# A DeltaNet recurrence with a gelu MLP on one core: the written-out order of all engines, loads, PSUM banks and filler matmuls, planned anew

## The chip, the cores and the metric

The kernel runs on one core of one Trainium2 chip. A core has five engines that each work through a queue of their own: PE (matrix products; loading its weights is shown apart as PEld), DVE (VectorE), ACT (ScalarE), POOL (GpSimd) and SP, which here only issues loads and copies. The metric is the device time of one execution in microseconds (us).

## The reference

A linear attention with a delta rule runs over 768 steps for 4 x 8 heads with 48 channels each; its output, laid out as 3072 tokens of 384 channels, goes through an MLP with a tanh gelu.

```python
k_n = k / (np.linalg.norm(k, axis=-1, keepdims=True) + 1e-06)
for t in range(S):                                  # S = 768
    y[:, :, t] = einsum('bhd,bhde->bhe', q[:, :, t], state)
    v_old = einsum('bhde,bhd->bhe', state, k_n[:, :, t])
    state = state + beta[:, :, t] * einsum('bhd,bhe->bhde', k_n[:, :, t], v[:, :, t] - v_old)
x = y.transpose(0, 2, 1, 3).reshape(3072, 384)
h = x @ w_in                                        # 384 -> 2048
g = 0.5 * h * (1 + tanh(sqrt(2 / pi) * (h + 0.044715 * h**3)))
out = g @ w_out                                     # 2048 -> 384
```

## The kernel before

The 768 steps are cut into 12 chunks of 64. For a chunk, k is squared and summed (`sq`, `ss`), a reciprocal norm is made (`sr`, `rn`), and k is scaled to `Kn` and transposed by PE into `KQT`, beside the transposed q. Products of k with itself and with q give the chunk's triangular matrices (`gram`: `G`, `DT`; `own`: the 16 x 16 and 32 x 32 blocks on the diagonal). The diagonal blocks are inverted by forward substitution in many small instructions (`solve8` on DVE for chunk 0; `solve` on POOL for chunk 1 and then for pairs of chunks), transposed back by DVE (`back`: `TB0`, `TB1`), spread into block matrices (`WB`, `DI`, by `exp`) and joined to the whole inverse `TT` by products (`inverse`: `ET`, then three products one after another). `state` then takes the recurrence one chunk on: `R` = old values minus v, `U` = TT times R, the new state `S`, and the chunk's output, which lands transposed in `x4` ("x" in the text). For most chunks some rows of x are moved by six small DMAs (`xm`).

The MLP works on tiles: chunks 0 to 3 are a tile each, chunks 4 to 11 are taken in pairs (8 tiles, t0 to t7). A first-layer group (`m1`, L1241) fills one PSUM bank by PE, and ACT makes the gelu of it into `gT` (L1243, 128x512). The second layer (`m2`, L1251) is issued in halves of 8 matmuls; its result goes through `osb` to the output by a DMA on ACT's queue.

All of this is recorded as 1277 operations and emitted in an order that is written out by hand in the string `ORDER` at the head of the file. An entry is a letter for the engine and the number of the operation: `p` PE, `v` DVE, `a` ACT, `g` POOL, `s` SP; `p224` is operation 224 on PE, the first MLP group. Some operations may run on either of two engines, and the letter chooses. An entry `w6.7` puts six matmuls on a constant tile `wz` (L414) into PE's queue, writing to PSUM bank 7: filler, whose result is not used. Each engine takes its entries in the order in which they stand in the string, one after another; an entry waits by semaphores for the operations that it reads from, for those whose buffers it overwrites, and, where it takes a PSUM bank, for the last users of that bank. `BANK` gives the bank of each PSUM handle, a digit each. Entries of different engines stand in one string, but only the order within each engine is kept on the chip.

```python
            o = ops[int(w[1:])]
            o.eng, o.end = names[w[0]], n
            assert o.eng in o.fns and o.deps <= seen and o.idx not in seen
            seen.add(o.idx)
            for h, k in o.alloc:
                b0 = self.bank_of[h] = int(BANK[h[1] - 1])
                for b in range(b0, b0 + k):
                    o.sync.update(bank_last[b])
                    bank_last[b] = tuple(self.users[h])
            self.orders[o.eng].append(o.idx)
```

Loads of k, q and v are issued on SP, in order, each behind the reads of the buffer that it fills (three buffers for k and v, one for q); four loads of W1 and four of W2 are issued on POOL, between its compute entries, once q of the first two chunks has landed (`WAFT`), with two more for the rows that hold the fourth part of a head (`W1x`).

Operations that the prediction follows, with their numbers: 61 (transposed beta), 82 and 84 (the two halves of chunk 0's square), 89 and 90 (halves of K0), 66 and 69 (the masks bM of chunks 0 and 1), 152 (own blocks of chunk 0), 156 and 155 (first sums of chunk 0's solve, L846 and L843), 177 (its last transpose), 186 and 187 (DI0), 189 to 203 (chunk 0's inverse on PE), 205 (R0, which reads v of chunk 0, `vf0`), 206 to 212 (its state), 218 and 219 (its x), 224 to 238 (first layer of tile 0), 240 to 246 (its second layer), 307 and 308 (WB of chunk 1), 312 to 326 (its inverse), 398 and 399 (own blocks of chunks 2 and 3), 401 (their transpose `Tt0`), 448 and 466 (first products of their inverses), 349 to 363 (first layer of tile 1), 365 (second layer of tile 1), 510 (of tile 2), 653 (an inverse product of chunk 4). Those numbered 122, 130, 390, 393, 593, 596, 786, 789, 973 and 976 scale k to K.

Of the kernel before, what the change touches and what calls it, by code (L numbers as in the profile page):

```python
# [18 lines left out]
v34 a50 g11 s49 v5 v0 g21 v46 a48 s47 g22 v6 g16 v8 v35 v41 g18 s54 v1 v4 a2 g13 g14 s55 g12 g19 v15 v45 s53 a26 v43  # L19
v33 v10 s56 v3 w6.7 p61 v36 v37 v9 v38 s51 v42 v7 v40 s52 a82 g84 v63 s60 a24 g20 v85 g17 a29 v39 v62 a30 a31 v83 a32  # L20
a23 v67 a86 s59 v70 a87 v64 v88 s57 a97 g75 v89 v65 g81 s58 w12.5 p91 v66 a98 p99 g90 v44 v92 g77 w1.4 p93 a103 v68
p100 v94 g72 g76 a101 s96 p152 v104 g74 v153 g73 a105 w1.7 p181 a106 a182 v107 v154 g108 v156 v155 g69 w8.3 p109 v157
v158 v159 a110 v160 v183 g80 s141 a102 v161 w4.5 p264 v162 v163 v164 p178 v265 a179 v165 g266 v166 a117 v167 v168 v169
v170 a25 a28 g267 a27 v171 g268 g269 v172 g270 g271 v173 g272 g273 v174 g274 g275 v175 g276 g277 v176 a185 g278 g279
s95 a184 v177 w29.3 p191 g280 p301 g281 v192 g282 a187 p189 v186 g283 v190 g284 a188 w1.5 p195 g285 v118 p193 g286
a196 g287 a194 p199 v71 g288 v180 p197 g289 a200 g78 a119 p203 v198 a120 g290 a205 p201 v121 g291 v204 v122 g79 a202
p209 a302 p206 g292 g293 s147 v207 a210 g294 g295 a125 v208 s140 v211 g296 w3.5 p215 v303 p216 g297 p217 s146 p304
v218 a219 p212 p123 v126 a305 g299 v298 a127 a128 v129 a133 v306 g130 v300 s115 v124 a213 s113 g400 w12.7 p131 v308
a309 s116 p398 v132 a311 s114 g603 v214 p399 a250 s111 p314 v401 a310 s112 a315 v251 s144 g402 s142 a375 v307 s143
g403 g404 w10.6 p312 v376 a135 s145 g405 p224 g406 s262 g407 p226 v377 a225 g408 v378 s263 v379 p328 a134 g409 v380  # L30
p228 v381 g410 v382 a313 s151 g411 v329 p136 g412 p137 s150 a229 g413 v383 p316 v138 p318 g414 s149 a317 v384 g415
p438 a227 v385 s223 p230 g416 v386 v139 a439 g417 s222 p232 a231 v387 g418 s148 v388 p320 a233 g419 v389 p459 v319
g390 s220 p234 a460 v440 s221 p322 a235 v321 p456 v461 p324 g420 a323 s396 a457 g393 p326 p441 s397 v327 a519 p236
v325 v458 p333 a442 g421 v520 p238 g422 a334 p391 g423 a253 v443 g424 p330 g425 a239 v331 p338 g426 p394 a252 v332
g427 v335 p339 v392 p340 g428 p341 a578 s259 p342 g429 p240 g430 v344 s260 g431 a343 g433 v579 a395 s258 p254 a237
g432 v580 p601 s345 v437 p602 s261 a444 v434 p241 s346 v462 s347 v604 p255 s348 a242 p349 s436 v256 g605 p351 a350
s435 v581 p644 v582 a352 p466 s531 v583 g521 p353 v584 a645 v585 s532 v445 p245 g522 a354 v646 a257 g606 v586 v587
g607 p355 g608 v464 a467 g609 p336 v588 v446 p448 g610 v337 p246 g611 a449 g612 v589 g613 v463 p523 g614 v590 a356
v591 p474 g615 v592 a247 p450 g690 a447 p357 v451 p359 v475 g593 p524 a360 p452 v525 a358 p468 g616 v453 a526 s599
p361 g596 v469 s600 p454 a362 p363 s527 v455 g617 v691 p476 s530 g618 p470 a477 g619 p480 s529 p594 g620 a364 p481  # L40
s528 g621 p478 a482 g622 p365 v479 s483 g623 a771 g624 s489 v471 p366 g625 s491 a595 v772 g626 s488 g627 g628 p533
a243 v773 s490 p662 v774 g629 p597 a244 v775 s492 g630 v776 p370 g631 a598 v777 s487 v778 g632 v779 g633 v780 s703
a367 g634 p371 v781 g636 v782 a692 s702 v783 v784 v785 g635 p794 v534 a372 a663 p795 v640 g786 a465 p493 v647 p495
v664 a494 g693 p472 v797 a496 p497 s792 g883 p499 v473 a498 s793 v637 p535 v648 s638 g796 p501 a536 v884 s699 p539
a502 p540 p641 g798 s486 v541 p694 a642 s639 p503 a500 v643 s700 g799 p695 a504 g800 p505 v696 g801 s548 p507 a506
s546 v697 p537 a665 s547 p651 g789 p659 v652 p509 s701 a508 s550 v538 a660 g802 p790 s549 g803 a374 p510 v661 g804
s698 a958 g805 v791 s551 g806 a249 v649 p837 g807 p669 v959 s484 p653 a248 g808 s485 p514 g809 a838 v654 g810 a668
g811 v670 a511 p515 g812 g813 v667 v839 g814 p552 g815 v960 a516 v961 p655 g816 v962 a553 p834 g817 v656 p677 a835
g818 p554 v963 g819 a650 v678 p556 g820 a555 g821 p657 v836 a557 g822 p558 v658 a886 g823 v666 g824 p679 g825 a559
# [26 lines left out]
a1276  # L76
"""
BANK = ("6031340340660141100441256766766777042000503073120036766677667154142444144220200367676676760000276766"
        "7676754202240042244430024042067667677676767676767024104052244440000220220666767676767676767661042024"
        "2242042530200022767767667676767676764000444440000044210001203141021031450102")  # L80


# [1257 lines left out]
```

## Time and profile before

| | before |
|---|---|
| time, median of 3 runs | 251.39 us (251.34 to 253.34) |
| profiled execution: span from first to last instruction | 249.4 us |
| profiled execution: time of its own | not given on the page; the median lies 2.0 us above the span |
| PE busy | 232.0 us (93%) |
| DVE, ACT, POOL busy | 161.4, 139.0, 118.6 us |
| mean granted TensorE clock | 0.986 |
| filler matmuls (L414) | 87 |
| HBM read, written | 20.64 MB, 4.72 MB |

The page lists the busy time of each engine, the span in 40 slices of 6.2 us with a digit for tenths of busy time, the granted clock of PE in the same slices, the share of the DMA engines, and the chain of waits, which is followed back from the last instruction. A line of a timeline has start, length, engine, line of the kernel, operation, output and input tiles, and in brackets what ended the idle time before it. A line of a table by stretch has the stretch, its length, then busy time and number of instructions for PE, PEld, DVE, ACT and POOL, the clock, the DMA share and GB/s.

### The profile page before, as it was taken

How to read it: one execution, taken by the hardware profiler on the slowest of the kernel's cores; microseconds unless marked ns; L12 is line 12 of the kernel's file. 1: busy time of each engine (PE TensorE's matmuls, PEld its weight loads, DVE VectorE, ACT ScalarE, POOL GpSimd, SP SyncE). 2: the span in 40 equal slices, each digit the busy share in tenths (PEclk: the TensorE clock that was granted, in tenths of full speed). 3: DMA queues.
4: the chain of work that ended last, by engine and by line, in shares of the span. 5: the costliest groups of instructions: out<-in, count | busy, mean ns of one | idle time of the engine just before them, and what ended most of it. 6: DMA issues, size and time to landing. Idle time of an engine off the chain costs nothing.

```text
span 249.4 us, 12386 instructions
## 1 busy us (share of the span) xinstructions
PE 232.0 (93%) x5637; PEld 155.0 (62%) x5637; DVE 161.4 (65%) x316; ACT 139.0 (56%) x262; POOL 118.6 (48%) x249
## 2 busy tenths in 40 slices
PE   7577896998999799999899999999999999999995
PEld 4334473587778658868766655666656665555562
DVE  6699989886799399896969653767772465100001
ACT  2744578587686466838564357535682247426600
POOL 3685796688389858588045589883000000000000
PEclk9999999799999799999999999999999999999999
DMA  6999969996740825550244000623135210000112
GB/s 157 209 196 168 159 116 211 159 214 107 184 87 19 192 52 112 122 137 7 57 111 91 5 20 23 149 57 63 37 76 134 78 37 3 8 11 32 66 63 96
DMA packets 64789, 23.84 MB, mean 96 GB/s; under 512 B 53600, under 2 KB 63840, under 8 KB 64736
## 3 DMA queue, kind: packets, MB, share of 16 engines
q1 hardware_dynamic: 58656, 14.89, 30.8%
q0 software_dynamic: 1056, 3.15, 7.3%
q10 hardware_dynamic: 5024, 5.02, 6.3%
q8 instruction: 44, 0.72, 1.2%
q14 instruction: 9, 0.07, 0.1%
HBM read 20.64 MB, written 4.72 MB: 102 GB/s over the span
## 4 chain that ended last, share of the span: by engine, by line
PE 81%; DVE 10%; DMA 2%; issue 2%; ACT 2%; POOL 0%; ACTq 0%; POOLq 0%
PE ps L267 76%; DMA kf<-in_k_dram 2%; PE ps L648 2%; PE ps L680 2%; PE ps L414 1%; DVE ss L603 1%; DVE WB L931 1%; ACT WB L915 1%; DVE TB L806 1%; DVE KQT L256 1%; DVE ps L846 1%; DVE Yf L251 1%; DVE Tt L837 1%; DVE btz L251 0%; DVE ps L786 0%
## 5 line engine op out<-in xcount | busy, mean ns | idle before, releaser
L260 ACT ACTIVATE gT<-ps 128x512 bf16<-128x512 f32 x96 | 55.9, 597 | 38.4 <-PE ps L267 36.8
L267 PE MATMUL ps<-x,W 128*128 128x256 bf16 (+1 forms) x384 | 72.2, 329 | 0.0
L267 PE MATMUL ps<-W,gT 128*128 128x384 bf16 x384 | 67.0, 328 | 0.0
L267 PEld LDWEIGHTS ps<-W,gT 128*128 128x128 bf16 x384 | 36.4, 98 | 23.9 <-issue 0.5
L267 PEld LDWEIGHTS ps<-x,W 128*128 128x128 bf16 x384 | 39.1, 115 | 16.3 <-issue 0.3
L762 POOL TENSOR_TENSOR Yf<-Yf,tmp 128x28 f32<-128x28 f32 (+13 forms) x84 | 28.8, 342 | 6.4
L759 POOL TENSOR_TENSOR tmp<-Yf 128x28 f32<-128x28 f32 (+13 forms) x84 | 28.1, 335 | 6.1
L251 DVE TENSOR_TENSOR TT<-ps,DI 128x768 bf16<-128x768 f32 (+2 forms) x30 | 20.2, 684 | 13.8 <-PE ps L267 13.5
L414 PE MATMUL ps<-wz 128*128 128x512 bf16 x87 | 23.3, 416 | 1.4 <-DVE wz L409 1.4
L251 POOL TENSOR_TENSOR Kn<-kf,rn 128x768 bf16<-128x768 f32 (+1 forms) x11 | 16.0, 1452 | 17.1 <-DVE rn L629 10.1
L267 PE MATMUL ps<-KQT 48*32 48x32 bf16 (+1 forms) x1152 | 18.7, 195 | 5.8 <-issue 2.7
L260 ACT ACTIVATE osb<-ps 128x384 f32<-128x384 f32 x18 | 8.8, 490 | 26.3 <-PE ps L267 26.3
L256 DVE COPY osb<-ps 128x384 f32<-128x384 f32 x6 | 3.2, 552 | 29.8 <-PE ps L267 29.8
L260 ACT ACTIVATE G<-ps 128x512 bf16<-128x512 f32 x24 | 14.3, 597 | 11.4 <-PE ps L267 7.7
L267 PEld LDWEIGHTS ps<-KQT 48*32 48x32 bf16 (+1 forms) x1152 | 13.6, 95 | 10.9 <-issue 5.0
L719 DVE TENSOR_TENSOR DT<-ps,mD 128x512 bf16<-128x512 f32 x24 | 16.3, 680 | 4.1 <-ACT G L260 4.1
L267 PE MATMUL ps<-TT,ET 64*64 64x32 bf16 (+1 forms) x768 | 16.4, 176 | 0.0
L267 PEld LDWEIGHTS ps<-TT,ET 64*64 64x64 bf16 x768 | 14.8, 109 | 2.2 <-DVE R L251 0.6
L414 PEld LDWEIGHTS ps<-wz 128*128 128x128 bf16 x87 | 8.7, 105 | 11.5 <-issue 3.0
L251 DVE TENSOR_TENSOR S<-ps,S 128x768 bf16<-128x768 f32 x10 | 9.5, 953 | 9.0 <-PE ps L267 8.9
L260 ACT ACTIVATE x<-ps 128x1024 bf16<-128x1024 f32 (+2 forms) x10 | 9.2, 916 | 8.1 <-PE ps L267 7.9
L251 DVE TENSOR_TENSOR R<-ps,vf 128x768 bf16<-128x768 f32 x11 | 10.4, 949 | 3.8 <-PE ps L267 3.8
(122 smaller groups left out, 333.2 us busy)
## 6 DMA issues: line engine op xcount, KB each, us to landing
qf<-in_q_dram SPq DMA_DIRECT2D x24, 192.0 KB, 4.4
kf<-in_k_dram SPq DMA_DIRECT2D x23, 192.0 KB, 4.9
vf<-in_v_dram SPq DMA_DIRECT2D x40, 96.0 KB, 3.2
out_dram<-osb ACTq DMA_DIRECT2D x16, 192.0 KB, 2.0
W<-in_moe_w_out_dram POOLq DMA_DIRECT2D x4, 384.0 KB, 6.7
out_dram<-osb ACTq DMA_DIRECT2D x16, 96.0 KB, 2.8
W<-in_moe_w_in_dram POOLq DMA_DIRECT2D x4, 192.0 KB, 8.7
vf<-in_v_dram SPq DMA_DIRECT2D x4, 192.0 KB, 11.3
```

The costliest lines, as they stand in the source:

```text
L251: return lambda e: e.tensor_tensor(out() if callable(out) else out, a() if callable(a) else a, b() if callable(b) else b, op)
L256: return lambda e: e.tensor_copy(out, a() if callable(a) else a)
L260: return lambda e: e.activation(out, a() if callable(a) else a, func)
L267: ins = t.matmul(out, lhsT, rhs, start=st, stop=sp_, skip_group_check=skip)
L414: ins = e.matmul(psum[:, b, :], wz[:, 0:128], wz[:, :], start=True, stop=True)
L603: op({"dve": 0.95 * w}, {"dve": lambda e, u=u: e.tensor_reduce(ss[j][:, u], sq[:, u, :], AX.X, ALU.add)}, reads=[f"sq{n}"], writes=[f"ss{j ...
L648: ins = e.transpose(o[:, a, j], Qn[:, n, a, j, :, :].rearrange("q h d -> q (h d)"), identB[:, :])
L680: ins = e.transpose(tb()[:, m, :], t[:, 2 * m:2 * m + 2, :].rearrange("p h d -> p (h d)"), identB[:, :])
L719: op(d_ps(512), {"dve": lambda e: e.tensor_tensor(dv, gview(1)(), md, ALU.mult)}, reads=[h] + MD, writes=[dn])
L759: sop(nb * s * w, lambda e, s=s, w=w, tv=tv: e.tensor_tensor(tv, yf[:, :, s:s + 1, 0:s].to_broadcast([128, nb, w, s]), Yv()[:, :, s + 1:16 ...
L762: sop(nb * s * w, lambda e, s=s, tv=tv: e.tensor_tensor(Yv()[:, :, s + 1:16, 0:s], Yv()[:, :, s + 1:16, 0:s], tv, ALU.add), [YN, TN], [YN])
L806: op({"dve": 0.58}, {"dve": lambda e: e.transpose(dst, src)}, reads=reads, writes=writes)
```

## The change

The strings `ORDER` and `BANK` are replaced. The 1277 operations, their operands and their dependencies stay as they are. What differs:

- the order of the entries on each of the five engines, the places of the loads among them, and the bank of most PSUM handles;
- the engine of 80 operations: 39 go from DVE to ACT, 20 from ACT to DVE, 10 from POOL to DVE, 2 from DVE to POOL, 5 from ACT to POOL and 4 from POOL to ACT;
- the filler: 87 matmuls in entries of 6, 12, 1, 1, 8, 4, 29, 1, 3, 12 and 10 become 68 in entries of 5, 15, 6, 4, 4, 4, 2, 18, 4, 3 and 3.

The string's lines up to about the first group of MLP tile 1, its end, and the banks:

```diff
@@ ORDER
-v34 a50 g11 s49 v5 v0 g21 v46 a48 s47 g22 v6 g16 v8 v35 v41 g18 s54 v1 v4 a2 g13 g14 s55 g12 g19 v15 v45 s53 a26 v43
-v33 v10 s56 v3 w6.7 p61 v36 v37 v9 v38 s51 v42 v7 v40 s52 a82 g84 v63 s60 a24 g20 v85 g17 a29 v39 v62 a30 a31 v83 a32
-a23 v67 a86 s59 v70 a87 v64 v88 s57 a97 g75 v89 v65 g81 s58 w12.5 p91 v66 a98 p99 g90 v44 v92 g77 w1.4 p93 a103 v68
-p100 v94 g72 g76 a101 s96 p152 v104 g74 v153 g73 a105 w1.7 p181 a106 a182 v107 v154 g108 v156 v155 g69 w8.3 p109 v157
-v158 v159 a110 v160 v183 g80 s141 a102 v161 w4.5 p264 v162 v163 v164 p178 v265 a179 v165 g266 v166 a117 v167 v168 v169
-v170 a25 a28 g267 a27 v171 g268 g269 v172 g270 g271 v173 g272 g273 v174 g274 g275 v175 g276 g277 v176 a185 g278 g279
-s95 a184 v177 w29.3 p191 g280 p301 g281 v192 g282 a187 p189 v186 g283 v190 g284 a188 w1.5 p195 g285 v118 p193 g286
-a196 g287 a194 p199 v71 g288 v180 p197 g289 a200 g78 a119 p203 v198 a120 g290 a205 p201 v121 g291 v204 v122 g79 a202
-p209 a302 p206 g292 g293 s147 v207 a210 g294 g295 a125 v208 s140 v211 g296 w3.5 p215 v303 p216 g297 p217 s146 p304
-v218 a219 p212 p123 v126 a305 g299 v298 a127 a128 v129 a133 v306 g130 v300 s115 v124 a213 s113 g400 w12.7 p131 v308
-a309 s116 p398 v132 a311 s114 g603 v214 p399 a250 s111 p314 v401 a310 s112 a315 v251 s144 g402 s142 a375 v307 s143
-g403 g404 w10.6 p312 v376 a135 s145 g405 p224 g406 s262 g407 p226 v377 a225 g408 v378 s263 v379 p328 a134 g409 v380
-p228 v381 g410 v382 a313 s151 g411 v329 p136 g412 p137 s150 a229 g413 v383 p316 v138 p318 g414 s149 a317 v384 g415
-p438 a227 v385 s223 p230 g416 v386 v139 a439 g417 s222 p232 a231 v387 g418 s148 v388 p320 a233 g419 v389 p459 v319
-g390 s220 p234 a460 v440 s221 p322 a235 v321 p456 v461 p324 g420 a323 s396 a457 g393 p326 p441 s397 v327 a519 p236
-v325 v458 p333 a442 g421 v520 p238 g422 a334 p391 g423 a253 v443 g424 p330 g425 a239 v331 p338 g426 p394 a252 v332
-g427 v335 p339 v392 p340 g428 p341 a578 s259 p342 g429 p240 g430 v344 s260 g431 a343 g433 v579 a395 s258 p254 a237
-g432 v580 p601 s345 v437 p602 s261 a444 v434 p241 s346 v462 s347 v604 p255 s348 a242 p349 s436 v256 g605 p351 a350
-s435 v581 p644 v582 a352 p466 s531 v583 g521 p353 v584 a645 v585 s532 v445 p245 g522 a354 v646 a257 g606 v586 v587
-g607 p355 g608 v464 a467 g609 p336 v588 v446 p448 g610 v337 p246 g611 a449 g612 v589 g613 v463 p523 g614 v590 a356
-v591 p474 g615 v592 a247 p450 g690 a447 p357 v451 p359 v475 g593 p524 a360 p452 v525 a358 p468 g616 v453 a526 s599
-p361 g596 v469 s600 p454 a362 p363 s527 v455 g617 v691 p476 s530 g618 p470 a477 g619 p480 s529 p594 g620 a364 p481
-s528 g621 p478 a482 g622 p365 v479 s483 g623 a771 g624 s489 v471 p366 g625 s491 a595 v772 g626 s488 g627 g628 p533
-a243 v773 s490 p662 v774 g629 p597 a244 v775 s492 g630 v776 p370 g631 a598 v777 s487 v778 g632 v779 g633 v780 s703
-a367 g634 p371 v781 g636 v782 a692 s702 v783 v784 v785 g635 p794 v534 a372 a663 p795 v640 g786 a465 p493 v647 p495
...
+v0 g11 s49 a50 v34 v46 g21 g16 s47 a48 g18 v3 g13 v35 v36 v43 g22 v37 v39 s52 v9 v33 g17 g12 v15 v38 v5 s51 w5.5 p61
+s60 v63 v7 v62 v64 g82 v4 v70 g14 s53 g84 v10 v41 s59 v83 v85 v1 v67 s56 v65 a86 a87 s55 a103 v88 g66 v40 v90 g19 g89
+v104 w15.5 p93 s96 p91 a94 s54 v92 a105 v68 s58 p152 a106 v107 v69 v153 g108 v44 s57 v154 v156 w6.5 p109 a110 s140
+v155 g72 a2 s95 a98 w4.5 p264 g20 g97 g73 s141 v265 v157 w4.5 p99 g266 v158 v159 p100 v160 v161 v162 a101 v163 v164
+g267 v165 v166 v167 a102 v168 w4.5 p178 g268 v71 p181 g79 v169 v170 g269 a32 a31 w2.5 p301 a26 g270 v171 a179 g271 a30
+v45 g77 a25 a24 v172 a205 g272 g78 a182 v173 g400 a23 a28 a27 v174 a302 a117 g273 v175 g274 v176 g275 a184 g276 v177
+g277 a185 w18.5 p189 g278 v180 g81 a186 v118 p191 g279 g603 v190 a119 a125 v192 w4.3 p193 g280 a187 g281 v194 g282
+v126 g283 w3.3 p195 g74 p304 v183 p197 g284 g285 v303 a198 g75 a29 a196 p201 a127 g286 a188 p199 g76 a120 a202 a200
+g287 p206 a128 a305 p203 g288 g80 a207 v204 v6 v42 p209 g289 v129 v306 g290 g291 v130 g292 v210 w3.2 p131 v208 g293
+a211 v121 a133 p215 g294 a250 v122 p216 g295 p217 g296 g299 s147 p123 v219 s146 p212 a124 v218 g297 v300 p224 a213
+v132 p228 v298 a225 s115 p398 v309 a308 s114 p399 v251 s113 a214 s116 v310 a229 s112 p232 v401 a375 s111 p226 a307
+v376 p328 g402 p314 a227 s262 a315 p230 v377 g403 v378 a135 g134 p318 v379 v380 v8 p312 v381 a319 v382 g404 s150 p136
+v383 g796 a313 v384 p137 s263 v385 v386 a233 s151 p316 v138 g405 a311 s148 p234 g406 v329 a317 s143 g407 a231 p322
+g408 v139 s149 a235 p320 g409 v387 a323 p459 g410 p438 a460 p236 v388 g411 v389 a439 v461 g412 p326 a321 g413 v390
+a237 p441 v327 p324 s397 v440 g414 a442 p456 p238 g415 s396 a519 v443 g416 p338 v325 a239 g417 p391 a457 g418 p240
+v392 a253 g419 v393 g420 a252 v458 g421 p333 p330 v520 g422 a334 s258 p601 a331 g423 s144 p339 a578 p394 g424 v332
+s260 g425 p241 v395 s142 g426 g427 v335 s145 v579 g428 p340 g429 s261 p341 g430 p342 s259 v580 v242 g431 g433 p602
+v581 a343 v582 a344 p254 v604 g432 p349 p255 a350 g605 v434 p351 a256 s435 p353 s436 v583 a352 v437 g606 p644 s220
+p336 g607 a645 v257 p245 g608 s221 g522 a444 v584 v585 s531 a354 v586 g609 v587 v445 g521 p448 a462 s532 v588 v646
+p355 a449 g610 p246 v446 s529 v589 v337 g611 a356 s528 g612 g981 s530 a465 v590 p466 v463 p474 s222 v464 a467 p450
+v591 v475 s527 g613 p359 s223 g614 v451 p523 a690 g615 p524 g616 v592 v247 a244 p468 g593 a525 p452 p357 v453 a526
+g617 s600 p594 v469 g618 s599 a447 p454 g619 a360 p480 g620 v455 p470 a358 s345 g621 p476 g622 v471 s347 p361 a477
+g623 v691 s346 p363 g624 a362 g625 p478 p481 g626 v479 p365 g627 a482 g628 v596 g629 a771 s702 g692 p533 s491 p472
+a364 v772 g630 s488 p662 g631 a249 p366 s489 a663 g632 v773 s490 v473 g633 a243 v534 g634 s487 a693 g636 p370 s492
+v664 a367 s348 g635 a595 v640 s703 p597 p371 a598 v774 v775 v776 v777 v778 p535 a372 v779 p539 v637 a647 p794 v648
...
@@ ORDER, its end (p1274 a1275 a1276 is the last of both)
-a1238 p1245 a1244 p1247 a1246 p1249 p1251 a1250 p1253 a1122 p1255 a1126 p1257 a1252 a1248 p1259 p1261 a1260 a1254
-p1128 a1256 a1258 p1262 v1129 a1130 p1265 a1263 a1264 p1266 p1269 p1270 p1273 v1271 v1267 a1268 p1274 a1272 a1275
+a1244 p1257 a1238 p1259 a1246 p1251 a1250 a1240 p1247 a1252 p1233 a1258 p1253 a1256 a1234 p1128 a1248 a1118 p1261
+a1122 a1254 a1129 p1265 a1260 a1130 p1269 p1270 p1266 a1271 a1272 p1262 a1267 p1273 v1263 a1264 a1268 p1274 a1275
@@ BANK
-BANK = ("6031340340660141100441256766766777042000503073120036766677667154142444144220200367676676760000276766"
-        "7676754202240042244430024042067667677676767676767024104052244440000220220666767676767676767661042024"
-        "2242042530200022767767667676767676764000444440000044210001203141021031450102")
+BANK = ("6730001422362525257070257666777776000332322323021457677677676004500444302024032067766776762202477777"
+        "6676753302245500045422204042266776767676676777667422034444400252222024002766677767676677777665400004"
+        "4444024302040104767766776766776766764022034242243042021404205713442571031023")
```

## The prediction

> **What bounds the kernel now.** I read the page first: busy time, slices, the chain of waits. Then a table of busy time by stretch, what PE waits for from 48 us on, and the timelines of PE, DVE, POOL and SP ahead of that.
>
> ```profile
> span 249.4 us, 12386 instructions
> ...
> PE 232.0 (93%) x5637; PEld 155.0 (62%) x5637; DVE 161.4 (65%) x316; ACT 139.0 (56%) x262; POOL 118.6 (48%) x249
> ...
> PE   7577896998999799999899999999999999999995
> ...
> PEclk9999999799999799999999999999999999999999
> ...
> PE 81%; DVE 10%; DMA 2%; issue 2%; ACT 2%; POOL 0%; ACTq 0%; POOLq 0%
> ```
> PE is filled from about the eighth slice on, and the chain has no other engine of weight after 43 us. The clock fell to 0.50 twice, 43.25 to 46.66 and 84.20 to 87.60.
>
> ```profile
> 43.10:48.20 5.10, 5.07 (x107) 2.72 (x108) 4.75 (x9) 2.74 (x6) 2.44 (x6) 0.67 0.99 184
> 48.20:69.50 21.30, 20.10 (x580) 16.77 (x580) 16.21 (x38) 15.38 (x29) 14.81 (x31) 1.00 0.81 162
> ```
> ```profile
> PE ps L267 <- issue: 3.7, 5, 1.3
> ```
> The last line is all that the matmuls of 48 to 145 us waited for: five gaps without a releaser, 3.7 us. So the end is set by one moment, that at which PE has real work in unbroken supply, and by what is then left. PE's own timeline shows that 43 to 48 us are not such a moment:
>
> ```profile
> 44.29 3.48 PE L414 MATMUL ps<-wz 128*128 128x512 bf16 x10
> 47.70 0.43 PE L267 MATMUL ps<-WB,G 64*64 64x48 bf16 x16
> 48.07 1.50 PE L267 MATMUL ps<-x,W 128*128 128x256 bf16 x12
> ```
> Ten matmuls on the constant, then one product of chunk 1, then the first MLP group (p224). Its x was ready at 36.8. It stands behind p312, which needs WB1_0 (v307, done 47.02), and DVE was late with that since its previous three entries ran against POOL's masks:
>
> ```profile
> 39.82 2.66 DVE L931 TENSOR_SCALAR WB<-TB,mBs 128x128 bf16<-128x128 bf16 x3
> 46.05 0.98 DVE L931 TENSOR_SCALAR WB<-TB,mBs 128x128 bf16<-128x128 bf16 x3
> ```
>
> **A measure of PE's work.** From the trace's signal times I take each PE entry's spacing from the entry before it, and the lower quartile of its kind as its unhindered time (0.65 us for a first-layer group, 1.30 for half a second-layer group, 0.29 to 0.61 for most attention groups). The 326 entries of real work come to 194.6 us. Before, 14.1 are done when p224 ends (48.92), 32.0 when p349 ends (69.50, first group of MLP tile 1), all at 246.49.
>
> **Part 1, chunk 0 up to its inverse (0 to 28 us): 0.3 to 0.5 us earlier.** Both squares go to POOL: 2 x 0.83 with a select of 0.3 between, from k's landing at 7.03, so the second sum waits until 9.1 instead of 8.0. POOL then has the mask product (1.27) and K0_0, which is done at 12.6 instead of 10.9 (DVE). The own blocks are at 13.9 against 14.28 all the same, as one copy moves to ACT and runs beside DVE's. Then a gain:
>
> ```profile
> 15.78 1.59 DVE L846 TENSOR_TENSOR ps<-Tt 128x256 f32<-128x256 f32 x1
> 17.29 1.48 DVE L251 TENSOR_TENSOR Yf<-Tt 128x256 f32<-128x256 f32 x1
> ...
> 15.24 1.84 POOL L251 TENSOR_TENSOR Kn<-kf,rn 128x768 bf16<-128x768 f32 x1 [0.65 <-DVE rn L613]
> 17.05 1.43 POOL L251 TENSOR_TENSOR bM<-btz,mS 128x512 f32<-128x512 f32 x1
> ```
> Each DVE entry ends 0.3 after the POOL entry that it overlaps; the product of twice the size took 0.69. So 0.45 each is fair, 2.1 us less. But bM1 comes onto DVE in front of them and meets the same POOL entry (13.7 to 15.2), and chunk 1's transpose (0.70) is put ahead of the solve: it starts at 18.95 against 18.80. One entry of 0.68 leaves the solve, a memset (0.38) and a change of sign (0.24) come in: end 25.2 against 25.68, last transpose (v177) 28.1 against 28.41.
>
> **Part 2, chunk 0's inverse and state (28 to 41 us): 4 us later.** DI0_0 (three ACT entries, 0.97) and chunk 3's square (0.83) now stand on ACT ahead of DI0_1: 31.75 against 29.91. Its products alternate between ACT and DVE with five other ACT entries between. On DVE two memsets, a reciprocal, DT1_1 and K3 (0.17, 0.17, 0.25, 0.63, 0.95: 2.2) stand ahead of U0_1, U3_0 of chunk 0. Walked entry by entry with these rows, x is ready at 41.6 against 36.8. On ACT and DVE an entry that needn't wait starts some 0.1 before the last one's end (32.00 behind the 0.38 from 31.72); seven such places make 0.7, so 40.9.
>
> **Part 3, the first MLP group: 7 us earlier.** It and a second one now stand directly behind chunk 0's state product, ahead of the own blocks of chunks 2 and 3 and of chunk 1's inverse, and no filler is behind them. p224 ends at 41.6 against 48.92, with 12.1 of work done against 14.1: credit 7.3 - 2.0 = 5.3. The filler itself (87 to 68 matmuls) gives nothing: ahead of this point it fills waits. The masks bM0, bM1 now run on POOL by 30 us, WB1 on ACT (0.97 each).
>
> **Part 4, 41 to 70 us: 1.5 to 2.1 given back.** ACT now has chunk 1's WB, S3, U and x: from gT0 to ET1_1 stand S3 0.72, gT 0.60, a square 0.83, WB 0.97 twice, gT 0.60, ET 1.09, so p318, which needs ET1_1, starts near 48.4 where PE arrives at 46.5 (with the half clock of 43 to 46.7 in it): 1.9 lost, and 0.2 at p316. 19.4 of work lie from p224 to p349; before, 17.9 from p224 to p349 took 20.6, a loss of 2.7. With the same loss and these waits p349 ends at 41.6 + 19.4 + 2.7 + 2.1 = 65.8; with a loss of 2.1 (chunk 1 no longer holds PE up) at 65.2. Before, the same 31.5 of work were done at 69.0. Gain 3.2 to 3.8; I take 3.5.
>
> **Part 5, the rest: nothing.** The order on PE stays within some ten places. Chunk 2/3's solve on POOL starts later (Tt0 at 47.7 against 45.3), but two of its K products (1.48 each) go to DVE, and WB0 had 6.6 us of slack ahead of p448. Before, from p349 to the end PE lost 177.0 - 162.6 = 14.4 us against its unhindered times, 1.4 of it in the second half-clock stretch; I take the same. The loads: k of chunks 1 to 3 ahead of q, W spread from 15 to 35 instead of 10 to 18 and 31 to 33. The last W1 piece is issued at 33.7; by the row of 8.7 from issue to landing it is there at 42.4, by the slowest, 11.2, at 45, by the quiet ones near 4.6 at 38.3; p224 starts at 40.9, so from nothing to 4 us of wait. I take nothing, since SP issues no load from 20 to 39. vf2 and vf3 move 10 to 18 places back on SP, behind q loads, and land 3 us or more ahead of R. The tail (copy, output DMA) is as before:
>
> ```profile
> 246.51 0.49 ACT L260 ACTIVATE osb<-ps 128x384 f32<-128x384 f32 x1 [7.31 <-PE ps L267]
> 247.03 0.34 ACTq L275 DMA_DIRECT2D out_dram<-osb  x1
> ```
>
> **Sum.** Span 249.4 - 3.5 = 245.9. The page gives no time of its own execution beyond the span; the median 251.39 lies 2.0 above it, and I keep that: 247.9 us.
>
> [...] Eight K products go from POOL to DVE (0.95 instead of 1.48). The row first: POOL's subtraction at 33.14 took 0.77 where its neighbours took 0.23 to 0.25, while such a DVE product ran (32.88 to 33.83). [...]
>
> **Rivals.**
> B, ACT takes the place of the waits (16%). 39 entries go from DVE to ACT, 20 back, four come from POOL. Walked with full row times, ACT is without a gap from 42 to 105 us; the groups p478, p653 and p510 then wait 0.4, 0.4 and 1.1 and others 0.4: 2.3 back, 250.2. For it: the many gelus (0.597) between which short copies must fit. Against: the 0.1 of overlap of part 2, 1.5 us over sixteen entries of such a stretch.
>
> C, vf0 late (18%), the slower side. R0 is now ACT's 21st entry, ahead of chunk 0's G0_1 and of the constants and WB; before, it was the 37th, at 32.36.
>
> ```profile
> 9.90 2.03 SPq L275 DMA_DIRECT2D vf<-in_v_dram  x2
> 12.04 10.31 SPq L275 DMA_DIRECT2D kf<-in_k_dram  x1
> ...
> DMA to landing us min/median/max: 2.5/3.4/18.6
> ```
> vf0 landed at 29.53; the next load's issue hung for 10.31 us while eight W loads were under way. If that repeats, R0 ends at 30.4 instead of 24.0, and everything from WB on shifts by 6.4: 254.3. From a landing at 26.7 on the gain is gone, from 29.2 on it is over 1% slower. Against: only two W1 loads are issued before 20 us, the first at 15.3. Six halves of k and four quarters of q had landed by 13.34; up to and with vf0 three halves more stand in the queue now, some 1.4 each, so 17.5, with W's share 18 to 21.
>
> D, half clock in the thin stretch (8%). From 25 to 31.5 PE has some 1.5 us of work. One more stretch of 3.4 at 0.50 costs up to 1.7, two 3.4: 249.6 to 251.3; I say 250.8. For: the two drops seen. Against: PE stood idle 2.77 at 8.2 to 11.0 at a clock of 1.00. [...]
>
> **How the numbers follow.** Forecast 58%: about 247.9, with parts 1 and 2 uncertain by 2 us either way; three quarters of it lie beyond 1% faster. 1% (2.5 us) is about what a measurement of this kernel can tell from no change. B is mostly within 1%, C slower, D within or slower. Faster 0.48 (0.45 of the forecast, 0.03 of B), same 0.29, slower 0.23. Low end 244.0: the whole credit of 5.3 kept (1.8 more), the second clock drop gone (1.4), and 0.7 of the doubt in part 2. High end 255.0: C, with 0.7 of the same doubt. The forecast's own range is 245.5 to 249.8.
>
> **What would show it.** Right: first MLP matmul at 39.5 to 43 us; no constant matmuls behind 39; v177 near 28; x of chunk 0 at 39 to 42.5, later than before; p318 waiting for ACT; p349 ending near 65.5. Wrong: R's entry on ACT starting behind 26; PE waiting for gT or DMA behind 48 in sum over 3 us more than before; a third clock drop; or p224 held for W.

## The result and the profile after

The changed kernel is slower: 268.81 us median (267.94 to 270.43) against 252.26 us (251.34 to 253.34) of the kernel before on the same chip, a ratio of 1.065 with a 95% interval of 1.057 to 1.072. The profiled execution took 267.94 us, its span is 266.1. Executions of one kernel lie up to 3% apart (264.4 to 272.6 us in the run spread below), in the kernel after the longer ones at a lower granted clock (267.94 us at 0.962, 270.43 at 0.943), so below the time of a kernel is the median of those within 1.5% of its quickest, and the range of all stands behind it. before, measured again beside every group of runs, had medians of 250.8 to 252.9, so 1 or 2 us between kernels of different groups tell nothing.

The page of the kernel after; in its slices a digit is a tenth, and of queue 8, which by the count below brings TensorE's instructions, the line has packets, MB and share of the DMA engines:

```profile
span 266.1 us, 12367 instructions
...
PE 237.0 (89%) x5618; PEld 156.2 (59%) x5618; DVE 150.0 (56%) x302; ACT 151.9 (57%) x303; POOL 109.7 (41%) x242
...
PE   8699678889878699998996989999989999999995
...
PEclk9979999799999799997997799999999999999999
...
q8 instruction: 44, 0.72, 1.1%
...
PE 70%; ACT 12%; DVE 7%; issue 6%; DMA 2%; POOL 2%; SPq 0%; ACTq 0%; POOLq 0%
```
TensorE's share fell from 93 to 89% and does not stay at 9 tenths. The clock now drops to 0.50 in five places (13.6, 47.7, 88.7, 122.8 and 143.3 us), and the chain of waits has 6% of "issue" where it had 2%. The same by stretch, and what TensorE's matmuls waited for from 48 us on:

```profile
48.20:69.50 21.30, 18.59 (x533) 14.36 (x533) 14.45 (x29) 13.76 (x29) 15.10 (x33) 0.93 0.64 138
69.50:88.60 19.10, 14.69 (x456) 11.90 (x454) 14.83 (x28) 14.03 (x27) 14.94 (x30) 1.00 0.65 129
88.60:144.90 56.30, 50.88 (x1564) 38.25 (x1564) 38.85 (x76) 34.85 (x62) 21.47 (x44) 0.93 0.34 73
```
```profile
PE ps L267 <- issue: 11.0, 12, 2.7
PE ps L267 <- DVE S L251: 1.1, 1, 1.1
```
Waits without a releaser ("issue" in the lines: nothing that the profile shows ended them) are 11.0 us in place of 3.7. The two longest, on TensorE's own timeline:

```profile
84.80 1.06 PE L267 MATMUL ps<-x,W 128*128 128x256 bf16 x8
88.51 0.93 PE L267 MATMUL ps<-x,W 128*128 128x256 bf16 x4 [2.65 <-issue]
...
141.67 0.21 PE L267 MATMUL ps<-DI,ET 64*64 64x48 bf16 x1
144.12 1.00 PE L267 MATMUL ps<-DI,ET 64*64 64x48 bf16 x31 [2.24 <-issue]
```
Both stop inside a group: the first behind two matmuls of six of p363, the second behind the first of 32 of p846, and the rest of the group came 2.65 and 2.24 us later, for the same operation. In the kernel an entry's semaphore waits stand ahead of its first instruction, so this is no wait for data. All eleven gaps of over 0.3 us without a releaser behind 43 us stand inside a group, behind 1 to 23 of its matmuls; all eight named ones of over 0.25 us stand ahead of a group's first matmul. I numbered TensorE's weight loads, matmuls and semaphore instructions (some 30 in a run) in order. Each gap of over 0.3 us without a releaser behind 43 us, in both kernels, ends at number 193 + 256n, give or take one: 1985, 2497, 3521, 5825 and 7105 before; those five and 1473, 5313, 6593, 9153 among others after. Queue 8 brings packets of 16384 bytes, 64 for each of 256 instructions, and its n-th packet goes with the n-th of these numbers. In the five gaps of before TensorE went on 1.2 to 1.7 us after the packet's bytes had landed, behind the eleven of after 1.1 to 1.7 us after. The gaps are waits for instructions.

An account of TensorE's time behind 43.1 us, in the measure of the prediction (us; half clock is half of the busy time at 0.50, where a matmul of 512 columns followed its like after 0.427 us, and after 0.216 at 1.00; "rest" is what entries take beyond their unhindered time without a visible gap). The sum of before reaches back to 41.8, where its named gap begins, and 1.2 us of its filler are half clock and stand in both columns, so that its rest is 1.2 more:

| | work | filler | gaps for instructions | named gaps | half clock | rest | sum |
|---|---|---|---|---|---|---|---|
| before | 182.5 | 3.4 | 3.7 | 1.4 | 3.4 | 10.3 | 204.7 |
| after | 181.2 | 0 | 12.6 | 5.0 | 8.1 | 13.2 | 220.1 |

The difference is 15.4 us: 8.9 more for instructions, 4.7 for the clock, 3.6 for named waits and 2.9 of rest, against 4.7 less work and filler behind that point. Set 4 us as what a block of 256 needs (fetch_alone, below, had 3.5 to 4.0): behind the early filler, the blocks with less work than that lack 23.7 us in sum after, 13.4 before; 13 blocks hold under 3 us of unhindered work against 6. The new order bunches attention groups (64 instructions in some 0.3 us).

### The profile page after: what moved, and what is told of

Same layout as the page of the kernel before. It is cut to its first block, busy times and chain, and to the rows that moved or that the text cites. A ratio compares the mean times of both kernels' runs of the same rounds, so it can differ in the third digit from the quotient of the medians.

```text
span 266.1 us, 12367 instructions
## 1 busy us (share of the span) xinstructions
PE 237.0 (89%) x5618; PEld 156.2 (59%) x5618; DVE 150.0 (56%) x302; ACT 151.9 (57%) x303; POOL 109.7 (41%) x242
## 4 chain that ended last, share of the span: by engine, by line
PE 70%; ACT 12%; DVE 7%; issue 6%; DMA 2%; POOL 2%; SPq 0%; ACTq 0%; POOLq 0%
PE ps L267 64%; PE ps L414 2%; PE ps L680 2%; ACT WB L915 2%; DMA kf<-in_k_dram 2%; PE ps L648 2%; ACT gT L260 2%; ACT ET L989 2%; ACT G L260 2%; DVE DT L719 1%; ACT KQT L260 1%; DVE KQT L256 1%; DVE Kn L251 1%; ACT sq L260 1%; DVE sr L626 1%
## 5 line engine op out<-in xcount | busy, mean ns | idle before, releaser
L267 PE MATMUL ps<-x,W 128*128 128x256 bf16 (+1 forms) x384 | 76.9, 343 | 4.0 <-issue 2.7
L762 POOL TENSOR_TENSOR Yf<-Yf,tmp 128x112 f32<-128x112 f32 (+13 forms) x84 | 29.8, 356 | 5.2
L759 POOL TENSOR_TENSOR tmp<-Yf 128x88 f32<-128x88 f32 (+13 forms) x84 | 28.7, 343 | 5.1
L251 POOL TENSOR_TENSOR Yf<-Tt,bM 128x512 f32<-128x512 f32 x5 | 6.4, 1285 | 47.2 <-DVE Tt L875 47.2
L260 ACT ACTIVATE osb<-ps 128x384 f32<-128x384 f32 x17 | 8.3, 492 | 28.1 <-PE ps L267 28.0
L267 PE MATMUL ps<-KQT 48*32 48x32 bf16 (+1 forms) x1152 | 17.9, 194 | 4.5 <-issue 2.7
L414 PE MATMUL ps<-wz 128*128 128x512 bf16 x68 | 19.9, 438 | 1.3 <-DVE pat L421 1.3
L267 PEld LDWEIGHTS ps<-TT,ET 64*64 64x64 bf16 x768 | 14.9, 109 | 3.5 <-issue 2.4
L260 ACT ACTIVATE KQT<-ps 128x1024 bf16<-128x1024 bf16 (+1 forms) x11 | 10.8, 982 | 10.0 <-PE ps L680 6.6
L989 ACT ACTIVATE ET<-ps,mE 128x256 bf16<-128x256 f32 (+1 forms) x30 | 11.4, 452 | 7.2 <-PE ps L267 7.1
L256 DVE COPY KQT<-ps 128x1024 bf16<-128x1024 bf16 (+1 forms) x14 | 9.3, 668 | 11.0 <-PE ps L680 7.2
L915 ACT ACTIVATE WB<-TB,mBs 128x256 bf16<-128x256 bf16 (+1 forms) x36 | 14.2, 464 | 0.0
```

The costliest lines, as they stand in the source:

```text
L251: return lambda e: e.tensor_tensor(out() if callable(out) else out, a() if callable(a) else a, b() if callable(b) else b, op)
L256: return lambda e: e.tensor_copy(out, a() if callable(a) else a)
L260: return lambda e: e.activation(out, a() if callable(a) else a, func)
L267: ins = t.matmul(out, lhsT, rhs, start=st, stop=sp_, skip_group_check=skip)
L414: ins = e.matmul(psum[:, b, :], wz[:, 0:128], wz[:, :], start=True, stop=True)
L759: sop(nb * s * w, lambda e, s=s, w=w, tv=tv: e.tensor_tensor(tv, yf[:, :, s:s + 1, 0:s].to_broadcast([128, nb, w, s]), Yv()[:, :, s + 1:16 ...
```

## Experiments

Theory F says that the supply of instructions and the clock behind it made the loss. Theory D says that operands and banks come late for the new order and the profile fails to name them (it is not rival D of the prediction). An operation behind `p` stands for TensorE's entry of that number; `w1` and three digits are that many matmuls of 48x32 by 32 columns.

**fetch_alone: the supply by itself.** Behind the last matmul of before:

```diff
+ w1512.0 w1512.0                   # 1024 matmuls of 48x32 by 32 columns
+ 6 x (w1112.0 w16.0)               # 112 of them, 16 of 512 columns
+ 4 x (w1104.0 w24.0)
```


> The kernel of before with work for TensorE alone behind its last matmul, on the zero constant: 1024 matmuls of 48x32 by 32 columns in a row (8 blocks of 256 instructions, a weight load and a matmul each); then six blocks of 112 such matmuls and 16 of 512 columns; then four of 104 and 24. Theory F (TensorE's instructions come in blocks of 256 by queue 8, whose 44 packets have 16384 bytes each, and no faster than one in about 3.4 us, the closest that two of these packets started in either trace): the first stretch takes 8 x 3.4 = 27 us or more, with a gap once in each 256 instructions; in the second, 16 x 0.22 + 112 x 0.01 = 4.6 us a block leaves gaps under 0.5 us or none; in the third, 6.3 us a block, none. Theory D (the gaps of the two kernels are waits for operands and banks that the profile fails to name): nothing is waited for here, the 64 matmuls of line 744 took 0.64 us, so the first stretch takes 1024 x 0.01 = 10 us without gaps of a period, 20 us at half clock.

TensorE's timeline, with all other engines at rest but the last output, and then one stretch of the mixed blocks:

```profile
246.82 1.06 PE L427 MATMUL ps<-wz 48*32 48x32 bf16 x107
250.28 1.18 PE L427 MATMUL ps<-wz 48*32 48x32 bf16 x128 [2.39 <-issue]
253.73 1.22 PE L427 MATMUL ps<-wz 48*32 48x32 bf16 x128 [2.27 <-issue]
257.74 1.25 PE L427 MATMUL ps<-wz 48*32 48x32 bf16 x128 [2.78 <-issue]
```
```profile
288.00:297.00 9.00, 9.00 (x257) 4.86 (x256) 0.00 (x0) 0.00 (x0) 0.00 (x0) 1.00 0.02 4
```
128 matmuls and 128 loads in 1.2 us, then 2.3 to 2.8 us of nothing, seven times, at 3.5 to 4.0 us a block; with some 4.5 us of work in a block (9.00 us for the 257 matmuls above) no gap at all. Between 251.8 and 279.1 us the clock stood at 0.50 with nothing on TensorE but these blocks and their gaps. F holds, with a mean of 3.8 us a block in place of 3.4. The three parts of it: behind a block with a wait the next packet starts 1.0 to 1.65 us after TensorE has entered the block ahead of it, takes 0.9 to 1.4, and TensorE goes on 1.2 to 1.55 after it has landed. In the mixed blocks it mostly starts 0.8 to 1.0 after.

**dup_small and dup_wide: the same work, many or few instructions.** On the kernel after:

```diff
- r.append((o, kk, kk, True, True, True))                 # own blocks, dup_small
+ r += [(o, kk, kk, True, True, True)] * 2
```
```diff
+ if gr > 1 and kt == 0:                                  # first MLP layer, dup_wide
+     r.append((<the same output, weights and x>, True, True, True))
```


> The kernel after in which each matmul of the own blocks (line 744, 64 of 32x32 by 32 columns to a group) is issued twice, with the same result: 768 weight loads and 768 matmuls more, in 12 groups. Its first stand in filler; 9 groups lie behind 43 us, where a group took 0.64 us, so that TensorE has 9 x 0.64 = 5.8 us more of work and 1152 more instructions. Theory F (instructions come in blocks of 256, one in 3.5 to 4.0 us at best, as the look with TensorE alone showed): 4.5 more blocks are 16 to 18 us of supply, of which roomy blocks take up some: 9 to 17 us more than 268.8. Theory D (operand waits, wherever the profile has no name for them): 4 to 7 us more.

> The kernel after in which the first matmul of each 256-column output in the first MLP layer of tiles 0 to 3 is issued twice, with the same result: 64 matmuls of 0.107 us, 6.8 us of TensorE work in much the same part of the run as in the run before this one, but 128 instructions in place of 1152. Theory F: the work falls partly into time in which the next block of instructions was awaited anyway: 1 to 5 us more than 268.8. Theory D: 6 to 8 us more, as each matmul adds its own time to a stream that waits for the same operands.

Measured: dup_small 286.2 us in one execution and 291.2 to 293.3 in three, 17 to 24 more than after; dup_wide 266.5 (265.3 to 267.3), 2.4 less, with 6.8 us more of work. Against before in its own group, dup_wide's ratio is 1.062 (1.054 to 1.070) and after's 1.065 (1.057 to 1.072), so no gain is shown, only that the kernel did not get slower. TensorE's busy time and its waits from 43 to 250 us, dup_small above (the execution of 291.2 us), dup_wide below:

```profile
PE 252.1 (87%) x6386; PEld 167.4 (58%) x6386; DVE 149.3 (52%) x302; ACT 152.4 (53%) x303; POOL 108.2 (37%) x242
```
```profile
PE ps L276 <- issue: 20.3, 14, 4.1
```
```profile
PE 244.2 (92%) x5682; PEld 163.6 (62%) x5682; DVE 151.2 (57%) x302; ACT 152.8 (58%) x303; POOL 109.6 (41%) x242
```
```profile
PE ps L276 <- issue: 4.8, 5, 2.1
```
5.8 us of small matmuls raise the waits for instructions to 20.3 us and the half clock to 15; 6.8 us of wide ones lower them to 4.8. D, which expected 4 to 8 us more from each, falls. F's bounds (9 to 17 and 1 to 5 us more) were too narrow on both sides, if only just for the execution of 286.2 us, as they left out the half clock that came with the gaps. dup_wide's 128 more instructions also move the later blocks, which the next run does alone.

**phase: the same stream, shifted by 128 places.** `w1064.5` (64 small matmuls) behind `w15.5`.

> The kernel after with 64 more matmuls (32 columns, constant, no use) behind the second filler, in the 1.5 us that TensorE is idle there: every later instruction stands 128 places further on in TensorE's stream, and nothing else changes. Theory F: gaps without a releaser end at instruction counts 193 + 256n as before, and so in front of other operations: those of 2.65 us ahead of p363 and 2.24 us ahead of p846 are not there, others come; their sum from 43 us on stays within 8 to 17 us (12.6 in the profile after), and the time within 261 to 274 us. Theory D: the same operations wait as long as before, counts 128 higher; time within 1 per cent of 268.8.

264.2 us (262.9 to 265.4). Gaps again end at 193 + 256n, now at other operations (p312, p470, p481, p694, p844, p747); the waits of 2.65 us in p363 and 2.24 in p846 are gone. Their sum is 9.2 us. The operations that waited by D do not wait any more. That 64 useless matmuls gain 4.6 us (ratio to before 1.042, 1.036 to 1.049) also says how much a time here depends on where the blocks fall. dup_wide, which comes to the same shift behind its 64 matmuls, is 2.2 us above phase, 4.9 by the two ratios to before: beside it, the wide work is not free.

**spread and spread_late, bunch, before_even and before_late: rearranged queues.** Each was found by a search over single moves, on the trace's durations and a supply of one block in some 3.7 us. An excerpt of TensorE's queue, spread against after (p569 is an MLP group, p979 and p980 are the own blocks ahead of the gap at 141.88 us):

```diff
- p787 p569 p864 p979 p980 p846 p723 p727
+ p787 p864 p846 p569 p979 p980 p723 p727
```


> The kernel after with the same operations on the same engines and banks; the queues of VectorE, ScalarE, GpSimd and the loads are untouched. Only TensorE's queue is rearranged: about 83 of its 337 entries stand up to 7 places from where they were, so that MLP groups (few and long instructions) lie more evenly between attention groups (many and short). Blocks of 256 instructions that are under 3 us of unhindered work fall from 13 to 7. Theory F: gaps of supply fall from 12.6 to 3 to 6 us and some stretches of half clock with them (8.1 us of cost now): 8 to 14 us less, 255 to 261 us. Theory D: operand waits are what they were, as the other engines do the same in the same order: 265 us or more.

> As the run spread, but TensorE's queue is that of the kernel after up to p349 (69.5 us), so that the early part with its idle stretches and half clock is not touched; only entries behind it are rearranged for an even spread. Theory F: from p349 to the end 193.6 us in the profile after; 186 to 189 us here (the run spread took 187.6), the whole 260 to 264 us. Theory D: 193 us, 267 to 270 us in all.

> The reverse, on the kernel before: only TensorE's queue is rearranged (some 65 of 337 entries, up to a dozen places), so that blocks of 256 instructions with under 3 us of unhindered work rise from 6 to 13, and so that by the durations of the trace no operand or bank is waited for longer in sum. Theory F: gaps of supply rise from 3.7 to about 10 us, and one or two stretches of half clock more: 258 to 266 us. Theory D: 250 to 254 us, as before.

> The kernel before, operations, engines and banks unchanged; the queues of TensorE, VectorE and ScalarE are rearranged by up to a dozen places so that blocks of 256 instructions take more even time and the durations of the trace leave fewer waits. Theory F: gaps of supply (3.7 us) and the half clock behind them mostly go: 246 to 250 us, faster than both kernels. Theory D: 250 to 254 us.

> As the run before_even, but up to p349 (69.5 us) every queue is that of before; only entries behind it are rearranged. Theory F: 2 us of the four gaps of supply behind that point, and the half clock of 84 us with its 1.7 us, go: 248 to 251 us. Theory D: 250 to 254 us.

spread 266.2 (264.4 to 272.6), spread_late 267.1 (one execution, 271.3 to 273.6 in three), before_even 264.1 (263.0 to 265.2), before_late 259.9 (258.6 to 262.7): all miss what F expected. The first two lie where D put them, the other two miss D as well. bunch 257.1 (255.5 to 261.5) lies between D's range and F's, and F's way failed in it: its gaps for instructions were 4.4 us, not 10. The accounts show why. Gaps and half clock fell as F said in before_even (1.8 and 0.3 us against 3.7 and 3.4), but named waits rose from 1.4 to 7.4 and the rest from 10.3 to 17.5. Part of that rest is a price that the search did not know: an entry behind a change between attention groups (weights of at most 64x64) and groups with weights of 128x128 takes some 0.09 to 0.10 us more than its kind's unhindered time, one without a change 0.00 to 0.03, where the matmuls are not merged. before makes 127 such changes behind 43 us, after 111, these five orders 143 to 154. So an even mix buys supply with 2 to 4 us of changes, and with later operands. None of the five beats the kernel before.

**engines: the 80 moves between engines undone.** `v` for `a`, `g` for `v` and so on in ORDER, at the places of after.

> The kernel after with each of the 80 operations that it runs on another engine (ScalarE, VectorE, GpSimd) put back to its engine in the kernel before; the order over all operations, the banks, TensorE's queue and the loads are those of after. Theory F (supply of instructions and the clock that follows it set the loss): within 1.5 per cent of 268.8. Theory D (ScalarE, with 303 instructions in place of 262, delivers late): 258 us or less.

272.1 us (268.9 to 272.5): the moves between engines aren't the cause; without them the order does slightly worse.

**merged_after and merged_before: fewer instructions in both.** In six attention steps two matmuls become one of twice the width, for example

```diff
+ if m % 2:
+     continue
- ... bank(h, hh)[.., D * m:D * m + D], KQT[i][rr, 0, m, cc], So[rr, 2 * m + a, 0:D]
+ ... bank(h, hh)[.., D * m:D * m + 2 * D], KQT[i][rr, 0, m, cc], So[rr, 2 * m + a:2 * m + a + 2, 0:D]
```


> The kernel after with two neighbouring matmuls made one of twice the width in six attention steps (lines 744, 968 for both of its uses from chunk 2 on, 1048, 1080, 1096): the second half of each output is computed from the wrong weights, so this part of the result is not the reference's. The columns that stream through TensorE, the queues, waits, banks and loads stay; some 2900 of the 9300 instructions behind 43 us go. To be read beside the same edit on before. Theory F (blocks of 256 instructions, one in 3.5 to 4 us at best, and the clock that drops after a wait for one): the difference of the two kernels, 16.4 us unedited, falls to 3 to 8 us, this kernel to 248 to 258 us. Theory D (order of operands, banks, other engines): both lose the same few us, the difference stays 14 to 18 us.

> The same merging of matmuls in the kernel before, with the same wrong weights in the second halves. Theory F: it has less supply to wait for (3.7 us of gaps), so it gains 3 to 8 us: 244 to 249 us. Theory D: 247 to 251 us, and 14 to 18 us under the same edit of after.

merged_after took 251.6 us in one execution and 255.6 to 255.9 in three, merged_before 246.9 (244.8 to 248.5). The difference of the kernels falls from 16.5 us to 4.7 with the execution of 251.6 us, to 8.8 with the median of all four. So supply with its clock is worth 8 to 12 us of the loss. F expected 3 to 8 left, D 14 to 18: F's range holds the one and nearly the other. What is left has names now. Waits of TensorE in the whole run, merged_after and then merged_before:

```profile
PE ps L276 <- ACT gT L269: 2.8, 6, 0.7
PE ps L276 <- DMA x<-x: 2.7, 4, 0.9
...
PE ps L276 <- issue: 2.2, 3, 1.0
PE ps L276 <- DVE S L260: 1.7, 2, 0.9
```
```profile
PE ps L276 <- DVE KQT L265: 3.0, 2, 2.4
...
PE ps L276 <- issue: 1.9, 1, 1.9
```
Waits for instructions are alike. merged_after also waits for gelus to leave their bank, for transfers of x and for the state, 17 times for over 0.25 us behind 43 us; named gaps there are 10.5 us against 3.0. The two profiled executions (251.6 and 248.5 us) differ by less than these 7.5 us, as the half clock cost merged_before 4.7 us there and merged_after 0.7.

**merged_engines: the merging, and the 80 moves between engines undone, on after.** If ACT's larger share made what merging leaves, 247 to 251 us were expected; if the order in which TensorE asks for operands and banks (theory W), 254 to 258. It took 261.9 us (261.6 to 265.8), more than either. With the engines of before the new order is slower again, as in the run engines, so ACT's share is not what costs; that W holds is not shown by this run.

**hyb_after_before, hyb_before_after, merged_hyb: which part of the order.** ORDER and BANK of one kernel up to p349, then of the other.

> The order, engines and banks of after up to and with p349 (first group of MLP tile 1), behind it those of before for all that is then left. Theory F+W (the loss is made behind p349: crowded blocks of instructions, and operands and banks that come late for this order): p349 near 69.5 us or some us earlier, then the 177 us of before: 249 to 254 us. Theory E (the early part of after leaves the other engines and the loads behind, and this is what costs later): 258 us or more.

> The reverse: before up to and with p349, after behind it. Theory F+W: 69.5 us and then 188 to 194 us, 262 to 269 us in all. Theory E: 250 to 256 us.

> The merged matmuls (second halves from the wrong weights) on hyb_before_after: before up to p349, after behind it (258.8 us unmerged, 5.5 above before). Theory F (the late part of after costs by supply alone): 245 to 249 us, level with merged_before (246.9). Theory W: 251 to 255 us, as the late part of after also waits for operands and banks.

265.8 us (264.0 to 267.0), 258.5 (258.0 to 262.8) and 253.3 (251.2 to 256.1). Neither theory of the first pair holds as put: both parts cost, the late one 2.2% (1.3 to 3.1%). The early part of after has p349 at 75.6 us in hyb_after_before, though the same order had it at 69.5 in the profile after. From 28 to 43.1 us, hyb_after_before above, after below:

```profile
28.00:43.10 15.10, 11.21 (x228) 6.80 (x229) 10.37 (x22) 9.68 (x29) 12.70 (x32) 0.74 0.83 148
```
```profile
28.00:43.10 15.10, 12.11 (x404) 8.81 (x404) 12.02 (x27) 11.52 (x31) 11.70 (x28) 1.00 0.84 156
```
The mean clock was 0.74 there (0.50 from 32.0 to 35.4 and from 38.8 to 49.0) and 1.00 here. phase, spread_late and dup_wide show the same drops on the same early order (phase with its 64 small matmuls more) (p349 at 71.8, 77.2 and 74.9). The late part of after costs 5.6 us behind the early part of before. merged_hyb is 6.4 above merged_before (4.9 if each is set against before in its own group): it waits at the same operations as merged_after, such as p509, p683, p704 and p723, with named gaps of 10.2 us behind 43 us against 3.0, and gaps for instructions of 1.6 against 1.9. What the late part costs in merged_hyb is operands and banks, not supply.

**warm and merged_warm: 16 more fillers in the early part.** `w18.5` to `w24.5`, `w2.5` behind p189, `w4.3` to `w5.3`, `w2.6` and three `w1.6` behind p201 to p203, `w3.2` to `w5.2`.

> The kernel after with 16 more filler matmuls (68 to 84) where TensorE is idle from 26.7 to 38 us; nothing else changes. Theory C (the early part of after, thinner in filler, mostly runs into half clock: 5 to 6 us until p349, as in spread_late and hyb_after_before, which had p349 at 77.2 and 75.6 us on the same early order): p349 at 66 to 71 us, 262 to 266 us in all. Theory F alone: p349 as in the profile after, 69.5 us, and 267 to 270 us, since 0 to 43 us cost only 1.7 us of clock there.

> The merged matmuls (second halves from the wrong weights) and the 16 more fillers on after. Theory C+F: both causes are relieved, 247 to 252 us, as merged_before (246.9) or a little above. Theory W (TensorE asks in an order in which operands and banks come late): 254 to 257 us, as merged_after (255.7).

warm took 261.2 us in one execution and 265.3 to 268.1 in three, less than after. But in the profiled one (261.2) p349 came at 71.0, no earlier than the 69.5 of the profile after, and what it gained lies behind that: 185.4 us from p349 to the end against 193.6. The 16 fillers are 32 instructions more and so also move the blocks, as in phase; what the early clock is worth by itself is not shown. merged_warm 255.1 (253.6 to 256.1), as merged_after mostly: the rest stays, as W said.

## Why the prediction was wrong

**Parts 1 to 3 held.** v177 ended at 27.88 (28.1 forecast), R0 began at 23.93 with vf0 landed at 18.8, so rival C did not come. The two DVE entries freed of POOL:

```profile
15.24 0.43 DVE L846 TENSOR_TENSOR ps<-Tt 128x256 f32<-128x256 f32 x1
15.58 0.42 DVE L251 TENSOR_TENSOR Yf<-Tt 128x256 f32<-128x256 f32 x1
```
x of chunk 0 was ready at 40.82 (40.9 forecast), p224 ended at 41.74 (41.6). That these sums came out so closely was in part luck: the clock was 1.00 from 28 to 43 us in this execution, and in those of four other runs on the same early order it was not.

**Part 4 failed on "the same loss".** p349 ended at 69.52, not near 65.5: behind p224 came gaps for instructions of 1.32, 0.71 and 0.87 us and a stretch of half clock at 47.74 (1.7), 4.6 us together. The 1.9 us at p318 did not come as forecast. ET1_1 was done at 49.06 (48.4 forecast), but TensorE was busy with p230, at half clock, until 49.55:

```profile
48.08 1.47 PE L267 MATMUL ps<-x,W 128*128 128x256 bf16 x6
49.48 0.53 PE L267 MATMUL ps<-DI,identB 64*64 64x384 bf16 x2
```
The head start came, and its credit was spent on supply and clock. How much of it would be left without them is not shown: with merging p349 is at 67.2 against 70.5 in merged_before, near the forecast 3.5, but from 28 us to p349 the half clock cost merged_before 6.4 us and merged_after 3.2, which is as much as that difference.

**Part 5, "the rest: nothing", is the step that failed.** It took over from before the loss of 14.4 us from p349 to the end. It was 193.6 - 162.6 = 31.0, 16.6 more, and these make most of the 20.2 us by which the span passed the forecast. From p349 to the end TensorE waited for instructions 9.2 us (before 2.6), the half clock cost 6.4 (1.7), named waits took 3.6 (none of over 0.15 us): 14.9 of the 16.6. I had read "the order on PE stays within some ten places" as harmless, and the five "issue" gaps as fixed. Ten places hold 256 instructions and more, so moves of that size decide whether a block holds 4 us of work or 1.35, the least in the new order, which ends at the gap of 2.24 us. The other part of the term, operands and banks for the order behind p349, I did not walk. Of the signs named ahead, the third clock drop came; waits for gT behind 48 us stayed at 1.0 us, and p224 was not held for W.

**Rivals.** B's ACT was not it (engines, merged_engines; its busy time from 42 to 105 us is 44.1 of 63 us). The prediction's D, half clock in the thin stretch, was right in kind but not in the profiled run; where it came, p349 stood at 71.8 to 77.2 us, 2 to 8 later and not 2.9, with longer waits for instructions in some. Against it the prediction had 2.77 us of idle at a clock of 1.00, from 8.2 us on; ahead of the two drops of before, 3.41 us hold 2.05 and 1.18 us of idle. In the traces of this case the clock changes on a grid of 3.41 us (in before at 43.25, 46.66, 84.21 and 87.62), and of 17 such windows at full clock behind 45 us with over 1.5 us of idle, in the traces of all kernels here but fetch_alone, 15 were followed by half clock, and none was idle throughout. Ahead of 45 us one of before was followed by full clock: 9.12 to 12.53, which holds 1.88 of the 2.77 us of idle. No rival had the supply of instructions, which cost 2.3 to 2.8 us a crossing in fetch_alone. With some 4.5 us of work in a block it left no gap there.

**What stays open.** The two parts, 8 to 12 us of supply with its clock and 5 to 9 of operands and banks, are measured by difference and not apart. Which move made the late operands was not tried one by one, and the early clock was not isolated. Nor is it settled why a packet's start lags: behind a block without a wait it came some 0.8 us after the crossing where the DMA engines were under 15% busy since, and some 2 us where they were over 90%.

## What to carry to other kernels

Count the instructions of an engine that runs near 90%, not only its time: here 256 of TensorE's took 3.5 to 4 us to arrive (fetch_alone), and the order that put attention's small matmuls together paid 12.6 us in gaps and 8.1 in half clock behind 43 us, where before paid 3.7 and 3.4. Look where a gap without a releaser stands: inside a group, and at the same instruction number in two kernels, it was a wait for instructions here. A planner that orders everything needs what was measured here in its costs: this floor, the 0.09 to 0.10 us of each change of tile form and the clock; the rearrangements here came from a search that did not know the price of a change, and lost there what they won in supply.

## What was unexpected of the hardware

- 64 more wide matmuls (6.8 us) did not make the kernel after slower, and 64 small ones without use, which move the blocks of instructions, made it 4.6 us faster.
- In fetch_alone 128 loads and 128 matmuls ran in 1.2 us, their supply took 3.5 to 4.0 us, with all other engines at rest but the last output.
- After a wait TensorE resumed 1.2 to 1.55 us after its packet had landed in fetch_alone, 1.1 to 1.7 in the two kernels.
- Of 17 windows of 3.41 us at full clock behind 45 us with over 1.5 us of idle, 15 were followed by one at 0.50.
- The same early order had p349 at 69.5 us in one execution and 77.2 in another (spread_late), mostly by the clock: from 28 us on half clock cost 1.7 and 10.0 us, waits for instructions 3.1 and 4.6.
